# P times V in eight 64x32 tiles over two banks, input sums formed earlier, two gate/up tiles in another phase

## The chip, the cores and the metric

One core of a Trainium2 chip runs the whole program in a single launch. The metric is the device time in microseconds (us), median of three runs. Work is spread over TensorE (matrix products, here PE, with its weight loads as PEld), VectorE (DVE), ScalarE (ACT), GpSimd (POOL) and SyncE (SP), which issues most transfers. Each engine works through its own instruction list in order.

## The reference, cut to what matters

One parallel block over S = 2048 tokens of width D = 640:

```
xn  = layernorm(x)                                   # no scale, no shift
q, k, v = split(xn @ wqkv)                           # 32 heads of 20
p   = softmax(where(0 <= i - j < 256, q k^T / sqrt(20), -1e9))
a   = (p @ v) @ wo                                   # sliding window of 256 tokens
h   = gelu_tanh(xn @ w_gate) * (xn @ w_up)           # 1728 wide
out = x + a + h @ w_down
```

All tensors are float32. The kernel forms the large products from a high and a low part of each operand (fp32r, "h" and "l"), in three products: high by high, low by high, high by low.

## The kernel before, in words

The work is staged as follows.

1. **LayerNorm stage.** Four chunks of 512 tokens are normalised and transposed into `xh` and `xl` (high and low part, five tiles of 128 rows), and V and the first query/key tiles are projected behind them. In this stage the order of work on GpSimd and SP is left to a planner that works from its own costs; the later stages have their order written out by hand on every engine that matters.
2. **Attention** (`attention`, L805). There are 32 units u = (group of 4 heads, chunk of 512 queries). A ramp of 12 slots (numbered -13 to -2) goes ahead of them, then each unit has 14 slots. In a slot the code emits, in order: deferred actions that are due (`tick`), row maxima (`max_pair`, two pairs at slots 0, 4 and 8, and two more after P times V at slot 0), exponentials (`exp_piece`, by the table `SCORES`), GpSimd items from a first-in-first-out list (`release`, up to two), and filler matmuls (`pull_fill`, `RATE`/14 of them a slot). An emitted instruction runs as soon as its inputs and its engine are free; a slot is a place in the order and not a time.
   - The filler (`filler`, L692) projects the remaining query/key and V tiles and computes gate/up tiles densely: 2 x 15 matmuls of 512 columns for each chunk of a tile, so 120 for a tile. `NFA` tiles are done here.
   - `max_pair` (L503) uses 64x32 tiles of the array, two rows of four, with two output banks, and VectorE reduces each bank (L527).
   - `exp_piece` (L568) makes a tile of P, keys by queries, for four heads; `clear` (L588) masks the diagonal and the window's tail on GpSimd (L595, L598). Three such tiles X, Z and Y (`pieces`, L549) belong to a unit.
   - `av_unit` (L601) multiplies P by V for unit u-1 at slot 0 of unit u. Four heads stand side by side as 128x32 tiles of the array, one output bank; ScalarE copies the bank out (L613) and SP stores it.
   - Six PSUM banks form a ring, taken in turn by maxima, exponentials and P times V (`bank`, L498).
   - `x_sums` (L729) forms sums of the normalised input that the next phase needs, for two chunk pairs p. A group of ten GpSimd subtractions and additions of 128x256 (L740) gives four tiles; eight groups are spread, one operation every two slots, over most of the units from slot 24 on. They work in two buffers (tag `tx`), each freed only when its store has landed.
3. **Seven-product phase** (`gate_up_pair`, L935). The remaining gate/up tiles use a Strassen-like scheme: for a pair of chunks 54 matmuls of 512 columns in place of 60.
4. **Down projection and output projection** (L1426 on), which uses a similar scheme.

## Time and profile before

| what | value |
|---|---|
| median of three runs (range) | 1046.38 us (1045.62 to 1047.34) |
| profiled execution, its own time | 1046.71 us |
| its span (first to last instruction) | 1045.0 us |
| granted TensorE clock | 0.999 |
| PE busy / DVE / ACT / POOL | 99% / 69% / 49% / 32% |

Attention takes from about 62 to 570 us of the span, the seven-product phase with its last tile from 570 to about 804 us, and the down projection the rest. Busy shares are averages over these stages. Durations of matmuls in the trace reach from start to a modelled end and overlap; the pitch from one to the next is read from the chain of waits.

### The profile page before, as it was taken

Reading aid. Unit: us, or ns where it says so; the run is one execution under the profiler, and the core shown is the slowest. Engines: PE = TensorE matmul, PEld = TensorE weight load, DVE = VectorE, ACT = ScalarE, POOL = GpSimd, SP = SyncE. Lnnn points to the kernel's source line nnn. Section 1 sums busy time; section 2 is a strip of 40 time slices with the busy share of each in tenths; the row PEclk is TensorE's granted clock in tenths of the full one; section 3 lists DMA queues with packets and bytes.
Section 4 is the critical chain, followed back from the end, with each engine's and each line's share of the span. In section 5 each row is a group of like instructions: output and inputs, shape, how many; then the busy total and the mean of one; then the engine's idle time right before and its main releaser. Section 6 shows DMA issues by size and latency. Waiting matters only on the chain.

```text
span 1045.0 us, 25814 instructions
## 1 busy us (share of the span) xinstructions
PE 1034.0 (99%) x9533; PEld 826.2 (79%) x9533; DVE 717.1 (69%) x2007; ACT 513.6 (49%) x1088; POOL 335.9 (32%) x511
## 2 busy tenths in 40 slices
PE   8999999999999999999999999999999999999998
PEld 8987666666677766666667888888888999999998
DVE  8745656666655556666663678877656888888887
ACT  4444666765665666555656522223324553333332
POOL 5222767766464458464634111110110000000000
PEclk9999999999999999999999999999999999999999
DMA  5552465545332355444322556677217864443342
GB/s 200 189 150 61 136 185 157 174 152 183 98 117 74 106 148 153 129 131 140 103 80 82 191 193 235 220 254 246 100 61 255 272 232 137 136 128 114 124 136 92
DMA packets 105192, 158.76 MB, mean 152 GB/s; under 512 B 15421, under 2 KB 60093, under 8 KB 105065
## 3 DMA queue, kind: packets, MB, share of 16 engines
q1 hardware_dynamic: 102680, 150.95, 45.1%
q10 hardware_dynamic: 2384, 6.16, 1.8%
q8 instruction: 75, 1.23, 0.5%
q14 instruction: 53, 0.43, 0.1%
HBM read 101.78 MB, written 54.92 MB: 150 GB/s over the span
## 4 chain that ended last, share of the span: by engine, by line
PE 89%; DVE 3%; DMA 3%; POOL 2%; SPq 1%; ACT 1%; issue 1%; DVEq 0%; POOLq 0%
PE ps_g L953 21%; PE ps L1220 21%; PE ps_d L110 19%; PE ps_e L582 7%; PE ps_v L110 7%; PE ps_o L609 7%; PE ps_m L523 4%; PE ps_g L110 1%; DMA qs<-qd 1%; SPq L494 1%; PE ps_t L181 1%; DMA qd<-pt 1%; POOL pt L259 1%; PE ps_d L356 1%; POOL wql L643 0%
## 5 line engine op out<-in xcount | busy, mean ns | idle before, releaser
L527 DVE CUSTOM_DVE_ANT_0 junk<-ps_m,mask 128x288 bf16<-128x288 f32 (+2 forms) x512 | 227.9, 445 | 155.0 <-PE ps_m L523 97.2
L584 ACT ACTIVATE P<-ps_e 128x512 f32<-128x512 f32 (+2 forms) x384 | 195.6, 578 | 59.8 <-PE ps_e L582 56.1
L1220 PE MATMUL ps<-wb,at 128*128 128x320 f32 x999 | 155.9, 309 | 0.0
L1220 PEld LDWEIGHTS ps<-wb,at 128*128 128x128 f32 x999 | 148.9, 188 | 0.2
L595 POOL TENSOR_SCALAR_AFFINE_SELECT P<-P 128x512 f32<-128x512 f32 x128 | 84.6, 663 | 139.1 <-ACT P L584 138.1
L582 PE MATMUL ps_e<-qs,ks 124*128 124x128 bf16 (+2 forms) x704 | 107.4, 277 | 0.6 <-DVE mx L527 0.5
L110 PE MATMUL ps_d<-xh,wqh 128*128 128x512 f32 x350 | 104.3, 410 | 0.0
L110 PE MATMUL ps_d<-xl,wqh 128*128 128x512 f32 x350 | 104.3, 409 | 0.0
L110 PE MATMUL ps_d<-xh,wql 128*128 128x512 f32 x350 | 103.9, 409 | 0.0
L1220 PE MATMUL ps<-wt,at 128*128 128x320 f32 x552 | 89.3, 309 | 0.4 <-DVE u L1058 0.4
L582 PEld LDWEIGHTS <-ks 124*128 124x128 bf16 x704 | 50.9, 98 | 46.5 <-issue 29.0
L609 PE MATMUL ps_o<-P,v 128*32 128x384 f32 (+2 forms) x1408 | 84.9, 386 | 0.7 <-POOL P L598 0.7
L1220 PEld LDWEIGHTS ps<-wt,at 128*128 128x128 f32 x552 | 82.9, 188 | 0.9 <-DVE u L1058 0.9
L598 POOL TENSOR_SCALAR_AFFINE_SELECT P<-P 128x512 f32<-128x512 f32 x112 | 70.3, 638 | 33.6 <-ACT P L584 33.6
L1174 ACT ACTIVATE at<-ss 128x512 fp32r<-128x512 f32 x59 | 37.3, 632 | 87.6 <-DVE ss L1058 87.5
L103 POOL TENSOR_TENSOR wql<-wr,wqh 128x640 fp32r<-128x640 f32 x11 | 17.6, 1607 | 174.8 <-PE ps_g L953 149.5
L609 PEld LDWEIGHTS ps_o<-P,v 128*32 128x32 f32 x1408 | 41.0, 109 | 40.5 <-issue 20.4
L110 PEld LDWEIGHTS ps_d<-xh,wql 128*128 128x128 f32 x350 | 63.9, 189 | 11.1 <-issue 0.4
L110 PEld LDWEIGHTS ps_d<-xl,wqh 128*128 128x128 f32 x350 | 63.8, 189 | 10.4 <-issue 0.2
L110 PEld LDWEIGHTS ps_d<-xh,wqh 128*128 128x128 f32 x350 | 63.5, 189 | 10.7 <-issue 0.2
L259 POOL TENSOR_TENSOR pt<-r,pt 128x512 bf16<-128x512 f32 x40 | 46.8, 1169 | 63.2 <-ACT pt L258 63.0
L613 ACT ACTIVATE ob<-ps_o 128x512 f32<-128x512 f32 x32 | 19.1, 598 | 86.3 <-PE ps_o L609 76.1
(194 smaller groups left out, 1846.8 us busy)
## 6 DMA issues: line engine op xcount, KB each, us to landing
hr<-hd SPq DMA_DIRECT2D x104, 128.0 KB
hd<-he SPq DMA_DIRECT2D x50, 256.0 KB
wr<-wgu SPq DMA_DIRECT2D x27, 320.0 KB
qs<-qd SPq DMA_DIRECT2D x64, 120.0 KB
ks<-kd SPq DMA_DIRECT2D x64, 120.0 KB
xi<-x SPq DMA_DIRECT2D x16, 320.0 KB
qs<-qd SPq DMA_DIRECT2D x64, 80.0 KB
ks<-kd SPq DMA_DIRECT2D x64, 80.0 KB
```

Of the source, the lines that this page charges most:

```text
L110: nc.tensor.matmul(ps, a(k), b(k), start=n == 0, stop=n == 3 * nk - 1)
L259: nc.gpsimd.tensor_tensor(out=pt[:, l, :], in0=r, in1=pt[:, 1, :], op=OP.subtract)
L523: nc.tensor.matmul(ps[32 * h:32 * h + 32, lo:hi], q[rows, j, q0:q0 + 32], keys, start=True, stop=True, tile_position=(64 * r, 32 * h))
L527: nc.vector.tensor_tensor_reduce(out=junk[:, 0:n], in0=ps[:, 0:n], in1=mask[:, 288 - n:288], scale=1.0, scalar=NEG, op0=OP.add, op1=OP.max ...
L582: nc.tensor.matmul(ps[:, col:col + n], k[0:QROWS, j, kc:kc + 128], q[0:QROWS, j, q0:q0 + n], start=True, stop=True)
L584: nc.scalar.activation(pt[:, j, lo:hi], ps[:, lo:hi], AF.Exp, scale=SCALE)
L595: nc.gpsimd.affine_select(out=a, in_=a, pattern=[[0, 4], [1, 128]], compare_op=OP.is_ge, fill=0.0, base=0, channel_multiplier=-1)
L598: nc.gpsimd.affine_select(out=a, in_=a, pattern=[[0, 4], [-1, 128]], compare_op=OP.is_ge, fill=0.0, base=-1, channel_multiplier=1)
L609: nc.tensor.matmul(o[32 * j:32 * j + 32, q0:q0 + n], v[:, w0_:w0_ + 32], pt[:, j, col:col + n], start=i == 0, stop=i == len(todo) - 1, ski ...
L953: nc.tensor.matmul(ps, i, j, start=first and n == 0, stop=n == len(work) - 1, skip_group_check=True)
L1174: nc.scalar.activation(hi[:, 3:7], s, AF.Copy)
L1220: nc.tensor.matmul(ps[bank][:, 0:HD], *work[bank][j], start=bank not in begun, stop=final[p, bank] == n and j == len(work[bank]) - 1, skip ...
```

## The change

- **P times V.** The 128 keys of a block become two halves of 64 keys on the two row halves of the array, each half of the sum in a bank of its own: 64x32 tiles, eight at a time. Each half takes only the 320 queries that its 64 keys can see, in place of 384 for 128 keys. The function `windows` pairs a window of the one half with one of the other. ScalarE copies both banks out, the second one into the unit's own P tile, which is no longer needed then; GpSimd adds the two one slot later, and the stores go one slot later too.
- **Sums of the input.** `x_sums` moves up in the file. For the first chunk pair it is called inside the LayerNorm stage (chunks 2 and 3), with two buffers of the tag `he`. For the second pair its 40 operations stand from slot -10 to slot 12, two to a slot; the ramp now releases two items a slot. Stores are deferred by one slot, not four.
- **Gate/up.** `NFA` goes from 4 to 2: two tiles leave the filler and are done in the seven-product phase.
- **Retiming.** `RATE` 34.05 to 26.6 filler matmuls a unit; the second half of V is projected after query/key tile 3; exponentials move from slot 0 to slots 2, 4, 6, 8 and 10.

```diff
-SCORES = {0: range(0, 1), 2: range(1, 5), 4: range(5, 7), 8: range(7, 9), 10: range(9, 12)}
-RATE = 34.05
-V1_AT = "gu", 0, 3
+SCORES = {2: range(0, 3), 4: range(3, 5), 6: range(5, 7), 8: range(7, 9), 10: range(9, 12)}
+RATE = 26.6
+V1_AT = "qk", 3, 3
...
-NFA = 4
+NFA = 2
...
-XS0, XSN = 24, 50
+XS0, XSN = -10, 6
...
+    def x_sums(p, k, half):
...
+            live[i] = (ap.tile([128, w], F32, name="tx", tag="tx") if p else
+                       hp.tile([128, C], F32, name="he", tag="he", bufs=2)[:, 0:w])
...
+            defer(1, lambda: nc.sync.dma_start(td[p][i][:, k, half * w:half * w + w], t))
...
+            if c > 1:
+                for half in range(2):
+                    for fn in x_sums(0, c - 2, half):
+                        fn()
...
+    def windows(c):
+        r = {}
+        for bi, ps in enumerate(pieces(c)):
+            for kb, col, q0, n in ps:
+                for h in range(2):
+                    first = 128 * (kb - 4 * c) + 64 * h
+                    lo = max(0, first) if kb else 0
+                    hi = min(C, first + 320)
+                    r[h, kb - 4 * c] = bi, kb, col + lo - q0, lo, hi - lo
+        pairs = [(0, 0), (-2, -2), (2, -1), (-1, 2), (1, 1), (3, 3)] if c else [(d, d) for d in range(4)]
+        return [[(h, *r[h, d]) for h, d in enumerate(p)] for p in pairs]
+
     def av_unit(u):
         g, c = divmod(u, NC)
-        o, v = bank("ps_o"), vtiles[g]
-        todo = [(pts[u, bi], *p) for bi, ps in enumerate(pieces(c)) for p in ps]
-        for i, (pt, kb, col, q0, n) in enumerate(todo):
-            assert (id(v), kb) in done, (u, kb)
+        halves, v = [bank("ps_o") for _ in range(2)], vtiles[g]
+        todo = windows(c)
+        for i, pair in enumerate(todo):
             for j in range(4):
-                w0_ = kb * 84 + 21 * j
-                nc.tensor.matmul(o[32 * j:32 * j + 32, q0:q0 + n], v[:, w0_:w0_ + 32], pt[:, j, col:col + n],
-                                 start=i == 0, stop=i == len(todo) - 1, skip_group_check=True,
-                                 tile_position=(0, 32 * j))
-        ob = ap.tile([128, C], F32, name="ob", tag="ob", bufs=1)
-        nc.scalar.activation(ob, o, AF.Copy)
+                for h, bi, kb, col, q0, n in pair:
+                    assert (id(v), kb) in done, (u, kb)
+                    rows, w0_ = slice(64 * h, 64 * h + 64), kb * 84 + 21 * j
+                    nc.tensor.matmul(halves[h][32 * j:32 * j + 32, q0:q0 + n], v[rows, w0_:w0_ + 32],
+                                     pts[u, bi][rows, j, col:col + n], start=i == 0, stop=i == len(todo) - 1,
+                                     skip_group_check=True, tile_position=(64 * h, 32 * j))
+        ob, other = ap.tile([128, C], F32, name="ob", tag="ob", bufs=1), pts[u, 2][:, 0, :]
+        nc.scalar.activation(ob, halves[0], AF.Copy)
+        nc.scalar.activation(other, halves[1], AF.Copy)
+        defer(1, lambda: nc.gpsimd.tensor_tensor(out=ob, in0=ob, in1=other, op=OP.add))
...
-        defer(3, store)
+        defer(4, store)
...
-    sets = [("qk", 1), ("qk", 2), ("qk", 3), ("gu", 0), ("qk", 4)]
-    sets += [("gu", f) for f in range(1, NFA)] + [("gu", NF - 1)]
+    sets = [("qk", i) for i in range(1, 5)] + [("gu", f) for f in range(NFA)] + [("gu", NF - 1)]
...
-        for i, (p, k, half) in enumerate((p, k, half) for p in range(NC // 2) for k in range(2) for half in range(2)):
-            for j, fn in enumerate(x_sums(p, k, half)):
-                at(XS0 + XSN * i + 2 * j, when_free, fn)
+        for i, (k, half) in enumerate((k, half) for k in range(2) for half in range(2)):
+            for j, fn in enumerate(x_sums(1, k, half)):
+                at(XS0 + XSN * i + j // 2, when_free, fn)
...
                 pull_max(2, now[0])
             flush()
+            release(2)
             pull_fill(2 * RAMP)
```

More of the change, by code (lines that the diff above doesn't have):

```diff
@@ L421, in first_chunk, with tile_of, pool, store @@
         return w0, w5, mv
+    def x_sums(p, k, half):
+        w = C // 2
+        a, b = (slice((2 * p + i) * C + half * w, (2 * p + i) * C + half * w + w) for i in (0, 1))
+        eh, el = xh.bitcast(F32), xl.bitcast(F32)
+        live = {}
+        def tile_of(i):
+            live[i] = (ap.tile([128, w], F32, name="tx", tag="tx") if p else
+                       hp.tile([128, C], F32, name="he", tag="he", bufs=2)[:, 0:w])
+            return live[i]
+        def pool(o, i, j, op):
+            nc.gpsimd.tensor_tensor(out=o, in0=i, in1=j, op=op)
+        def store(i):
+            t = live[i]
+            defer(1, lambda: nc.sync.dma_start(td[p][i][:, k, half * w:half * w + w], t))
+        def s1():
+            pool(tile_of(1), eh[:, k, b], eh[:, k, a], OP.subtract)
+        def s2():
+            pool(live[1], live[1], el[:, k, b], OP.add)
+        def s3():
+            pool(live[1], live[1], el[:, k, a], OP.subtract)
+            store(1)
+        def s4():
+            pool(tile_of(2), eh[:, k + 2, b], live[1], OP.subtract)
+        def s5():
+            pool(live[2], live[2], el[:, k + 2, b], OP.add)
+            store(2)
+        def s6():
+            pool(tile_of(4), eh[:, k + 2, a], live[2], OP.subtract)
+        def s7():
+            pool(live[4], live[4], el[:, k + 2, a], OP.add)
+            store(4)
+        def s8():
+            pool(tile_of(3), eh[:, k + 2, b], eh[:, k, b], OP.subtract)
+        def s9():
+            pool(live[3], live[3], el[:, k + 2, b], OP.add)
+        def s10():
+            pool(live[3], live[3], el[:, k, b], OP.subtract)
+            store(3)
+        return s1, s2, s3, s4, s5, s6, s7, s8, s9, s10
     v0 = []
```

38 lines of the change are left out of this document (removed).

## The prediction, made before the changed kernel was timed

> **What bounds the kernel now.** I read the page's busy shares first, then the stages in windows, then the chain of waits.
>
> ```profile
> PE 1034.0 (99%) x9533; PEld 826.2 (79%) x9533; DVE 717.1 (69%) x2007; ACT 513.6 (49%) x1088; POOL 335.9 (32%) x511
> ...
> PE 89%; DVE 3%; DMA 3%; POOL 2%; SPq 1%; ACT 1%; issue 1%; DVEq 0%; POOLq 0%
> ```
>
> ```profile
> 62.00:570.00 508.00, 504.23 (x6479) 341.20 (x6478) 299.20 (x1169) 308.27 (x681) 286.53 (x445) 1.00 0.43 129
> 570.00:804.00 234.00, 234.00 (x1035) 193.76 (x1034) 165.61 (x275) 77.17 (x143) 24.90 (x17) 1.00 0.55 189
> ```
>
> The columns of the windows are span, then busy time of PE, PEld, DVE, ACT and POOL. TensorE is busy in attention and in the seven-product phase alike, at the full clock, so a product that is saved is worth its own time, as long as nothing else comes late. The second view of the same fact is the chain in order of time, here a stretch of attention and the seven-product phase (start, length, what):
>
> ```profile
> 101.64 0.63 ACT pt L258
> 102.27 1.47 ACT P L584 x3
> ...
> 103.80 0.64 POOL P L595
> 104.44 0.60 POOL P L598
> ...
> 105.08 1.07 PE ps_o L609 x16
> ...
> 115.96 2.28 PE ps_d L110 x10
> 118.24 0.36 PE ps_m L523 x20
> 118.61 2.75 PE ps_o L609 x48
> 121.35 0.37 PE ps_m L523 x16
> ...
> 583.30 220.37 PE ps_g L953 x972
> ```
>
> Matmul follows matmul, with one exception to keep in mind: at 102 to 105 us, the end of unit 0, P times V waits for exponentials (ACT) and then for GpSimd's masks. Whatever makes GpSimd late at that place is paid in full.
>
> **The change, part by part.**
>
> *A. Two gate/up tiles move.* The filler loses 2 x 120 matmuls at 2.28/10 = 0.228 us: 54.7 us. The seven-product phase gains 2 x 2 x 54 = 216 at 220.37/972 = 0.2267 us: 49.0 us. Gain 5.7 us. Their weight loads, vector work and stores move with them into a stage where DVE is busy 166 of 234 us, so I cost these at nothing; if that cover failed, a tile's matmuls would still be 24.5 us each.
>
> *B. P times V.* A unit with c > 0 streams 12 passes (a float32 product takes two) over 1536 x 2 = 3072 columns in 2.75 us: 0.895 ns a column. The new pairs stream the longer of two windows: 320+128+256+192+320+128 = 1344, twice 2688 columns, 2.41 us; if the two halves can run apart, each has 1280, that is 2.29 us. For c = 0 it is 1152 before and 1088 (or about 1024) after. Saved: 24 x 0.34 + 8 x 0.11 = 9.1 us at the least, 24 x 0.46 + 8 x 0.23 = 12.9 us at the most; I take 11. This supposes that eight 64x32 tiles run side by side. The row maxima already work so:
>
> ```profile
> 512.17 0.32 PE L523 MATMUL ps_m<-ks,qs 60*32 60x288 bf16 x8
> ...
> 512.17 0.44 PE L523 MATMUL ps_m<-ks,qs 60*32 60x288 bf16 x16
> ...
> 509.06 0.45 PE L523 MATMUL ps_m<-ks,qs 60*32 60x32 bf16 x32
> ...
> 512.17 0.14 PEld L523 LDWEIGHTS <-qs 60*32 60x32 bf16 x16 [0.20 <-issue]
> ```
>
> The first eight end 0.12 us before the second eight (0.44 - 0.32): 288 columns in 0.12 us is the time of one stream, so eight did run at once, over two row halves and two banks. Matmul count itself is cheap: 32 took 0.45 us where 16 with the same columns in all took 0.44. The Trainium skill speaks against the change here: "TensorEngine Tiling (Array Packing)", section Instruction Overhead, gives some 60 cycles for every matmul and says that a dimension which is already small should give no tiling factor. By 60 cycles at 2.4 GHz, 25 ns, the 32 matmuls above would take 0.8 us; the trace has 0.45, so I don't follow it in the sum, and keep it as a rival.
>
> *C. Fewer changes of tile shape.* P times V is emitted between two bursts of maxima. Before, the shapes are 64x32, 128x32, 64x32; after, all three are 64x32. The last row above shows what a change costs: the weight loader sat idle 0.20 us, with nothing to wait for, before the maxima that follow P times V; some 0.1 us of it is the last pass still streaming (128 columns at 0.895 ns). Two such borders a unit at 0 to 0.1 us: 0 to 6.4 us over 32 units; I take 0.15 us a unit, 4.8 us. (The skill's same page, Key Properties, says that a change of tiling mode drains the engine; the idle 0.20 us agrees.)
>
> *D. The sums, ahead of the units.* Rows for GpSimd, from lists of single lines and from the timeline:
>
> ```profile
> L740 POOL TENSOR_TENSOR tx<-tx,xl x48: 723/733/1109, 121.0 to 513.9; 128x256 f32<-128x256 f32 x48
> ...
> 27.94 3.03 DVE L190 TENSOR_TENSOR xl<-ps_t,xh 128x512 fp32r<-128x512 f32 x5
> ...
> 40.02 0.61 POOL L467 MEMSET xi<- 128x288 f32 x2 [1.24 <-PE ps_t L181]
> ...
> 45.72 0.44 POOL L473 COPY mask<-xi 32x288 f32<-32x288 f32 x1
> ...
> 68.65 1.17 POOL L259 TENSOR_TENSOR pt<-r,pt 128x512 bf16<-128x512 f32 x1 [9.32 <-ACT pt L258]
> 69.77 3.09 POOL L103 TENSOR_TENSOR wql<-wr,wqh 128x640 fp32r<-128x640 f32 x2
> ...
> 103.62 1.28 PE L609 MATMUL ps_o<-P,v 128*32 128x384 f32 x16
> ```
>
> Follow GpSimd's list from slot -10 to the masks of tile Y of unit 0, which stand at slot 11. It holds 4 low parts of projections (1.17 us), the two low weights (3.09), 36 of the second pair's 40 operations (0.74 each, 26.6) and the 6 masks of unit 0 (0.6 apart, 3.6): 38 us. It cannot start before 68.65, when the first of them has its input; so it ends at 106.7 without a single wait. TensorE wants the masks earlier than that: P times V stood at 103.62, unit 0 loses 7.45 filler matmuls (1.7 us), and the first pair of windows (384 columns, two passes) takes 0.7: 102.6. GpSimd is 4 us late, and TensorE, which works in order, stands. To this come the waits for buffers: each group of ten reuses its two buffers four times, and the store must have landed:
>
> ```profile
> POOL tx L740 <- DMA td<-tx: 4.8, 3, 4.3
> ...
> PEld ps_o L609 <- POOL P L598: 3.8, 13, 1.0
> ...
> PEld ps_o L609 <- POOL P L595: 1.9, 4, 0.7
> ...
> PEld ps_o L609 <- POOL tx L740: 1.2, 6, 0.2
> ```
>
> (waiter, releaser: total us, times, longest). 1.6 us a wait at a looser spacing; with one a group not hidden, 4 x 1.3 = 5 us. I take 9 us. Ends: GpSimd's whole work from 28.5 us, when the first pair's inputs exist, is masks 5, eight low parts 9.4, weights 3.1, 76 operations 56, masks of unit 0 3.6: 77 us, done at 105.6 if it never pauses, so 3 us is the least. The most: of the 40 us between 28.5 and 68.65 some 30 are free, and the first pair needs 29.6 plus 4 waits of 1.6; 6 us spill over, 16 in all. Queued behind the late masks are the last four sums, their stores, and behind these on SP the loads of unit 3's queries; they come due at slot 4 of unit 1 and are inside the upper end. What moves out of the units frees GpSimd of 80 x 0.74 / 32 = 1.9 us a unit and takes away the six waits of the last row: gain 1 us.
>
> *E. The tail of P times V and the ring.* New on GpSimd is the addition, 128x512, between 1.17 us (the subtraction above) and two 128x256 (1.48 us), less than the 1.9 freed, and one more ScalarE copy:
>
> ```profile
> L613 ACT ACTIVATE ob<-ps_o 128x512 f32<-128x512 f32 x32 | 19.1, 598 | 86.3 <-PE ps_o L609 76.1
> ...
> 512.55 0.46 DVE L527 CUSTOM_DVE_ANT_0 junk<-ps_m,mask 128x288 bf16<-128x288 f32 x1 [0.80 <-PE ps_m L523]
> ...
> 513.16 0.46 DVE L527 CUSTOM_DVE_ANT_0 junk<-ps_m,mask 128x288 bf16<-128x288 f32 x1
> ```
>
> 0.6 us on an engine that is busy 308 of 508 us; ScalarE and GpSimd hide both. What they do not hide is that a unit gets shorter, about 15.8 to 13.7 us, while VectorE's sixteen maxima at a pitch of 0.61 us stay (9.8 us, with the rest some 11.5). Exponentials at slot 6 now take the banks of maxima from slot 4. TensorE gets there after 0.37 (maxima) + 0.35 (two exponentials) + 0.87 (two slots of 1.9 fillers) + 0.1 = 1.7 us, and the third maximum is reduced after 1.83: a wait of 0.1 us when VectorE is free, 0.8 when one operation of 0.7 us stands before it. Also the time between the last exponentials and Y's masks shrinks by 4 x 0.12 us of filler and 0.23 of earlier windows, where 5.7 us of waits are seen now (17 times). Between 0 and 0.5 us a unit, 0 to 16 us; I take 5, near the seen waits.
>
> *Sum.* -5.7 - 11 - 4.8 + 9 - 1 + 5 = -8.5 on a span of 1045.0: 1036.5. The profiled execution took 1046.71, 1.7 more than its span, and lies 0.3 above the median: about 1038.
>
> **The rivals.**
>
> *R1, slower: VectorE and the ring bind.* Place: slots 6 and 8 of every unit. It decides from (22.5 - 9)/32 = 0.42 us a unit. With 0.8 us, one other vector operation before the maxima each time, it is 26 us: 1059. For it: some 11.5 of 13.7 us of VectorE in a unit, and only six banks. Against: VectorE still waited for maxima (0.80 in the row above) and fillers stand between.
>
> *R2: GpSimd is not late, or TensorE regains it, and the ring holds.* D and E at their low ends: 1046.4 - 22.5 + 3 = 1027. Against it: the in-order count above.
>
> *R3: the burst eats the gain.* D at 16, with E at 5: 1045; no change to be told. For it: the chain already runs through GpSimd at 103.80.
>
> *R4: the eight don't run side by side*, because float32 differs from the maxima's bf16: P times V then takes 4.6 us a unit, 57 us lost: above 1100. R5: a floor per matmul, the skill's page above. With 25 ns, a pass of eight takes at least 0.2 us; the passes over 128 and 192 columns (0.115 and 0.172 us) grow, 0.4 us a unit, 10 us in all: 1048.
>
> **How the numbers follow.** Forecast 0.46 (own range 1032 to 1044), R2 0.20 (1023 to 1032), R3 0.14 (1043 to 1050), R1 0.14 (1049 to 1063), R4 0.03, R5 0.03. All terms at their low ends give 1024, at their high ends 1063. With 1026 to 1053 some 0.16 is left out. A measurement of this kernel tells 0.2%, 2.1 us, from no change: faster is below 1044.3, forecast, R2 and a little of R3, 0.70; slower above 1048.5, R1 and R4, 0.17; between 0.13.
>
> **What would show it.** A: the seven-product phase holds 1188 matmuls at about 0.227 us. B: P times V of a unit takes 2.3 to 2.4 us on the chain; 2.75 or more refutes B, and two separate groups of four would show R4. C: the idle time of the weight loader beside P times V goes below 0.1 us. D: TensorE waits for a mask (L595 or L598 of before) once, at 102 to 112 us, for 3 to 16 us, with GpSimd busy from 70 us on; no such wait refutes D. E: waits of scores or exponentials on the vector engine's maxima, each under a microsecond, 5 us in all; over 13 us gives R1. The forecast is wrong if neither D nor E is seen, or if attention shrinks by less than 50 us of its 508.

## The result: 1075.4 us, 2.7% slower, and the profile after

The changed kernel takes 1075.41 us (median of four runs, 1074.54 to 1075.85) against 1046.72 for the kernel before, timed beside it: a ratio of 1.0274, 95% interval 1.0256 to 1.0292. The forecast was 1038 us. The profiled execution took 1074.54 us with a span of 1072.8, 27.8 us longer than before.

The page of the changed kernel, busy shares, chain and granted clock:

```profile
PE 1037.1 (97%) x10917; PEld 852.0 (79%) x10917; DVE 731.3 (68%) x2029; ACT 523.1 (49%) x1120; POOL 374.7 (35%) x527
...
PEclk9989999999999999999999999999999999999999
...
PE 82%; DVE 5%; POOL 4%; DMA 4%; ACT 3%; issue 2%; SPq 1%; DVEq 0%; ACTq 0%; POOLq 0%
```

TensorE's share of the chain fell from 89% to 82%, and one of the forty slices, the one in which attention starts, no longer has the full clock. The chain of waits at the end of attention gives the split by stage (start, length, what), here the first piece after attention in the kernel before, and then in the changed one:

```profile
569.65 13.65 PE ps_g L110 x60
```

```profile
548.10 13.92 PE ps_g L110 x60
562.02 269.47 PE ps_g L973 x1188
```

Attention ends at 548.10 where it ended at 569.65: 21.5 us earlier, and the forecast had 57.5. The rest of the kernel is 49.4 us longer, and the forecast had 49.0. So all of the miss lies in attention. The windows of the changed kernel (span, then busy time of PE, PEld, DVE, ACT, POOL, then granted clock) show where TensorE is idle:

```profile
62.00:548.00 486.00, 459.04 (x7653) 327.65 (x7651) 286.16 (x1149) 304.59 (x691) 303.53 (x438) 0.98 0.43 128
...
62.00:82.00 20.00, 12.15 (x88) 9.39 (x87) 6.33 (x21) 4.37 (x14) 16.38 (x23) 0.74 0.39 123
98.00:108.00 10.00, 7.34 (x67) 6.93 (x67) 3.88 (x16) 2.29 (x13) 9.36 (x12) 0.83 0.65 199
122.00:130.00 8.00, 5.97 (x93) 3.80 (x101) 3.91 (x12) 2.66 (x5) 7.46 (x10) 0.79 0.42 120
```

The first of the short windows in the kernel before:

```profile
62.00:82.00 20.00, 20.00 (x210) 15.82 (x209) 10.17 (x45) 6.19 (x19) 5.39 (x4) 1.00 0.52 158
```

TensorE was busy for all of its 20 us, with 210 matmuls at the full clock; now it holds 88. In all three short windows GpSimd (the fifth busy time) works for 82 to 94% of the time. The chain and the lists of single lines say who waits for whom. Chain of the changed kernel:

```profile
67.91 0.73 POOL he L435
69.45 2.23 DMA ks<-kd
71.82 0.51 PE ps_m L581 x15
72.33 6.04 PE ps_d L110 x16
78.74 3.40 PE ps_d L110 x14
...
112.42 0.64 POOL P L653
...
121.76 0.73 POOL tx L435
122.48 0.59 POOL P L653
123.07 0.60 POOL P L656
123.72 1.58 PE ps_o L680 x38
```

SyncE's queue and TensorE in the timeline of the changed kernel; brackets give the idle time before an instruction and what ended it:

```profile
67.05 1.94 SPq L439 DMA_DIRECT2D td<-he  x2
69.05 1.11 SPq L552 DMA_DIRECT2D ks<-kd  x3
71.98 1.84 SPq L439 DMA_DIRECT2D td<-he  x2
73.87 1.10 SPq L552 DMA_DIRECT2D qs<-qd  x3
```

```profile
71.82 0.52 PE L581 MATMUL ps_m<-ks,qs 60*32 60x32 bf16 x27 [7.85 <-DMA ks<-kd]
...
100.66 1.51 PE L110 MATMUL ps_v<-wvh,xh 128*128 128x320 f32 x5 [2.82 <-DVE r L273]
...
123.72 1.59 PE L680 MATMUL ps_o<-P,v 64*32 64x320 f32 x47 [3.03 <-POOL P L656]
```

What SyncE itself waited for from 44 to 84 us (waiter, releaser: us in total, times, longest):

```profile
SPq L439 <- POOL he L435: 19.3, 14, 3.9
```

Read together: the sums of the first chunk pair (tile `he`, L435) run on GpSimd in the LayerNorm stage, from 27.5 to 81.3 us. Each store of a sum (L439) waits on SP's queue for GpSimd. Behind these stores, in the same queue, stand the loads of the first keys and queries (L552). These loads wait for nothing of their own: the last three for the first keys are issued at 69.05 us, as soon as the store ahead of them is out, where the kernel before had issued all six by 49.0. TensorE stands 7.85 us, and its score matmuls go on at 71.8 us; before, the first ones came at 62.4. The 16 filler matmuls after that take 6.04 us, 0.378 us each on average, where 0.228 is normal: the clock records have a granted share of 0.50 from 66.8 to 77.0 us. At 100 us VectorE's `r` (L273) has waited 5.5 us for GpSimd, and TensorE waits for `r`; at 123 us TensorE waits for GpSimd's masks. Each time the clock drops again. The first P times V starts at 119.7 us; before it started at 103.6.

The other thing to see is P times V itself (chain pieces, then the weight loads of the first):

```profile
305.92 3.00 PE ps_o L680 x61
...
332.77 2.21 PE ps_o L680 x60
```

```profile
306.40 1.95 PEld L680 LDWEIGHTS ps_o<-P,v 64*32 64x32 f32 x84 [0.53 <-DVE mx L585]
```

Where nothing is in its way, a unit's P times V takes 2.21 us on the chain, and 2.27 from its first matmul to the next instruction. In 18 of the 32 units P times V or its weight load waits for VectorE to read one of the four maxima that stand just ahead of it in the same slot, 8.2 us in all. So one of its two banks was last used by such a maximum, and P times V takes up to 2.9 us or starts up to 0.65 us behind the last maximum instead of 0.06.

### The profile page after: what moved, and what is told of

Read it like the earlier page. It is cut to its first block, busy times and chain, and to the rows that moved or that the text cites. A ratio compares the mean times of both kernels' runs of the same rounds, so it can differ in the third digit from the quotient of the medians.

```text
span 1072.8 us, 28727 instructions
## 1 busy us (share of the span) xinstructions
PE 1037.1 (97%) x10917; PEld 852.0 (79%) x10917; DVE 731.3 (68%) x2029; ACT 523.1 (49%) x1120; POOL 374.7 (35%) x527
## 4 chain that ended last, share of the span: by engine, by line
PE 82%; DVE 5%; POOL 4%; DMA 4%; ACT 3%; issue 2%; SPq 1%; DVEq 0%; ACTq 0%; POOLq 0%
PE ps_g L973 25%; PE ps L1240 20%; PE ps_d L110 12%; PE ps_e L640 7%; PE ps_o L680 6%; PE ps_v L110 5%; PE ps_m L581 3%; DVE junk L585 2%; DMA qs<-qd 2%; ACT P L642 1%; POOL he L435 1%; PE ps_g L110 1%; POOL tx L435 1%; POOL pt L259 1%; DMA ks<-kd 1%
## 5 line engine op out<-in xcount | busy, mean ns | idle before, releaser
L680 PE MATMUL ps_o<-P,v 64*32 64x320 f32 (+5 forms) x2816 | 85.8, 349 | 5.0 <-POOL P L656 3.6
L110 PE MATMUL ps_d<-xh,wql 128*128 128x512 f32 x270 | 85.9, 424 | 0.0
L110 PE MATMUL ps_d<-xh,wqh 128*128 128x512 f32 x270 | 85.4, 422 | 0.0
L110 PE MATMUL ps_d<-xl,wqh 128*128 128x512 f32 x270 | 83.8, 415 | 0.0
L581 PE MATMUL ps_m<-ks,qs 60*32 60x96 bf16 (+5 forms) x3008 | 68.1, 246 | 16.1 <-DMA ks<-kd 7.8
L680 PEld LDWEIGHTS ps_o<-P,v 64*32 64x32 f32 x2816 | 62.7, 106 | 22.8 <-DVE mx L585 6.8
L581 PEld LDWEIGHTS <-qs 60*32 60x32 bf16 x3008 | 34.3, 90 | 51.2 <-issue 43.9
L1002 ACT ACTIVATE hr<-hr 128x512 f32<-128x512 f32 x22 | 13.9, 632 | 111.4 <-DVE hr L976 111.4
L973 PE MATMUL ps_g<-xl,wqh 128*128 128x512 f32 x198 | 66.3, 389 | 0.0
L973 PE MATMUL ps_g<-xh,wqh 128*128 128x512 f32 x198 | 66.3, 389 | 0.0
## 6 DMA issues: line engine op xcount, KB each, us to landing
hr<-hd SPq DMA_DIRECT2D x104, 128.0 KB
```

Source lines behind the costliest of these rows:

```text
L110: nc.tensor.matmul(ps, a(k), b(k), start=n == 0, stop=n == 3 * nk - 1)
L581: nc.tensor.matmul(ps[32 * h:32 * h + 32, lo:hi], q[rows, j, q0:q0 + 32], keys, start=True, stop=True, tile_position=(64 * r, 32 * h))
L680: nc.tensor.matmul(halves[h][32 * j:32 * j + 32, q0:q0 + n], v[rows, w0_:w0_ + 32], pts[u, bi][rows, j, col:col + n], start=i == 0, stop=i ...
L973: nc.tensor.matmul(ps, i, j, start=first and n == 0, stop=n == len(work) - 1, skip_group_check=True)
```

## The experiments

All runs below the first row were timed in three rounds (w5 in five) beside the kernel before, which had medians of 1046.0 to 1046.3. "End" is the end of attention in the profiled execution. That execution was the longest of its run in e1, e4, e5 and y2, 2.3 to 3.8 us above the median, and in w1 1.5 us below it, so "end" and what is read from these traces are off by about as much.

| run | what it is | us (range) | ratio, 95% interval | end |
|---|---|---|---|---|
| after | the change | 1075.4 (1074.5 to 1075.9) | 1.0274 [1.0256, 1.0292] | 548.1 |
| e2 | before + early sums | 1065.4 (1064.1 to 1069.2) | 1.0186 [1.0158, 1.0214] | 588.4 |
| e8 | before + second pair early | 1052.9 (1052.3 to 1054.2) | 1.0068 [1.0051, 1.0084] | 575.1 |
| e1 | after, sums as before | 1073.6 (1070.0 to 1077.4) | 1.0259 [1.0230, 1.0289] | 549.5 |
| e3 | before + P times V | 1052.6 (1051.0 to 1053.0) | 1.0055 [1.0040, 1.0070] | 574.1 |
| e5 | e3 + new slots of exponentials | 1048.9 (1048.0 to 1052.5) | 1.0035 [1.0020, 1.0049] | 572.7 |
| e10 | after, P times V as before | 1076.3 (1074.4 to 1077.3) | 1.0286 [1.0270, 1.0301] | 550.2 |
| e9 | after, P times V ahead of maxima | 1109.9 (1109.6 to 1112.1) | 1.0613 [1.0597, 1.0629] | 582.9 |
| e4 | before + two tiles moved | 1062.1 (1059.6 to 1064.5) | 1.0149 [1.0126, 1.0171] | 538.3 |
| e7 | e4, sums late | 1051.2 (1050.0 to 1051.7) | 1.0046 [1.0031, 1.0061] | 524.4 |
| y2 | e4, sums spaced | 1051.8 (1050.8 to 1054.0) | 1.0048 [1.0033, 1.0063] | 527.8 |
| x_pvgu_late | after, sums late | 1066.1 (1065.2 to 1066.7) | 1.0190 [1.0175, 1.0205] | 539.5 |
| y1 | after, sums spaced | 1058.3 (1056.1 to 1061.9) | 1.0117 [1.0096, 1.0137] | 532.0 |
| w2 | e5, sums late | 1046.0 (1044.4 to 1049.2) | 0.9999 [0.9988, 1.0011] | 567.6 |
| w1 | e5, sums spaced | 1042.1 (1040.5 to 1045.4) | 0.9965 [0.9955, 0.9975] | 563.3 |
| w5 | before, sums spaced | 1043.8 (1043.2 to 1045.0) | 0.9976 [0.9966, 0.9986] | 566.0 |

### The early sums: e2, e8, e1

**e2_sums_only.** The kernel before with the change's two edits to the sums (the first pair in the LayerNorm stage, the second ahead of the units):

```diff
-XS0, XSN = 24, 50
+XS0, XSN = -10, 6
...
+            if c > 1:
+                for half in range(2):
+                    for fn in x_sums(0, c - 2, half):
+                        fn()
...
-                at(XS0 + XSN * i + 2 * j, when_free, fn)
+                at(XS0 + XSN * i + j // 2, when_free, fn)
...
```

> The kernel before with the early sums alone (P times V, the gate/up split and the exponentials' slots as before). Theory S: 20 us slower than before, 1060 to 1070, and the same waits for key loads and masks in the first 125 us. The prediction's step D alone (only the burst of GpSimd ahead of unit 0's masks, 9 us): 1055.

Measured: 1065.4, 19.4 us over the kernel before, as theory S had it. Waits of TensorE in this run (waiter, releaser: us in total, times, longest):

```profile
PE ps_m L581 <- DMA ks<-kd: 7.8, 1, 7.8
PE ps_o L679 <- POOL P L656: 4.6, 1, 4.6
PE ps_v L110 <- DVE r L273: 3.6, 2, 3.0
```

The first P times V starts at 119.2 us, the next 22.2 us later where 14.9 is normal, and the units after that are as before. The prediction's step D, 3 to 16 us, is only in the second row. The first row, the largest, stands at a place that the prediction had not considered.

**e8_second_pair_early.** The same with only the second pair early; the first pair is spread over the units, nothing is added to the LayerNorm stage. The edit against e2:

```diff
-            if c > 1:
-                for half in range(2):
-                    for fn in x_sums(0, c - 2, half):
-                        fn()
...
+        for i, (k, half) in enumerate((k, half) for k in range(2) for half in range(2)):
+            for j, fn in enumerate(x_sums(0, k, half)):
+                at(24 + 50 * i + 2 * j, when_free, fn)
```

> The kernel before with only the second pair's sums ahead of the units, as the changed kernel has them; the first pair's sums are spread over the units as before, none stand in the layernorm stage. With both early 1065.4 us were measured, 19.4 more than before. Theory L (most of the loss comes from the first pair: its stores stand on SP's queue ahead of the loads of the first keys, TensorE stands 8 us and then has half the clock for 10 us): the first score matmuls come when they came in the kernel before, and what is left is GpSimd's lateness for the masks of unit 0, 3 to 8 us and perhaps one more stretch of half clock: 1050 to 1056 us. Rival D (the burst ahead of unit 0's masks is the loss, as the prediction has it, and larger): 1060 to 1066 us, with the same waits for GpSimd's masks and about 3 units that start late.

Measured: 1052.9, 6.7 us over. Theory L holds. Waits and a window:

```profile
PE ps_o L674 <- POOL P L651: 4.6, 1, 4.6
```

```profile
110.00:114.00 4.00, 2.88 (x35) 1.15 (x36) 0.47 (x2) 0.60 (x1) 3.84 (x7) 0.50 0.60 167
```

One wait for the mask of unit 0, at 106 to 111 us, is step D as predicted. The clock records have 0.50 from 108.2 to 115.0 us, so that the four microseconds behind the wait run at half clock, which costs some 2 us: together with the wait's 4.6 that is the 6.7. The other 12.5 us of the 19.4 come with the first pair in the LayerNorm stage. That they come through SP's queue is read from the queue's own waits above; the queue alone was not changed in any run.

**e1_sums_back.** The changed kernel with the sums spread over the units as before.

```diff
-XS0, XSN = -10, 6
+XS0, XSN = 24, 50
...
-            if c > 1:
-                for half in range(2):
-                    for fn in x_sums(0, c - 2, half):
-                        fn()
...
```

> The changed kernel with the sums of the input placed as before (all eight groups spread over the units). Theory S (the early sums hold up the start: in the trace of the changed kernel the first P times V comes at 119.7 to 123.7 us, 20 us after the 103.6 of before, with a wait of 7.9 us for the first key loads, 3.0 us for masks, 2.8 us behind a vector operation, and half-clock stretches): about 1055 us, 1052 to 1058, with the granted clock back at 1.0 near the start. Rival (the start is lost for another reason, or is made up later): 1070 or more.

Measured: 1073.6, the rival's 1070 or more. The theory that the place of the sums explains the miss falls here as far as it was a sum of parts: the start is right again, but stretches of half clock appear at 168, 199 and 404 us instead, and TensorE's waits for the queries' loads rise from 4.8 to 10.2 us. With the sums in the units something else is as dear. The next runs look for it.

### P times V: e3, e5, e10, e9

**e3_pv_only.** The kernel before with the new `windows` and `av_unit`, nothing else.

```diff
-        o, v = bank("ps_o"), vtiles[g]
+        halves, v = [bank("ps_o") for _ in range(2)], vtiles[g]
...
-                                 tile_position=(0, 32 * j))
+                                     skip_group_check=True, tile_position=(64 * h, 32 * j))
```

> The kernel before with P times V in eight 64x32 tiles alone. The prediction's steps B, C and E: 11 us faster, 1035. Theory R (the second bank of P times V is taken from maxima of the same slot, which VectorE has not reduced, and the ring runs short elsewhere): the saving is eaten and more; from the stretch 124 to 548 us of the changed kernel, which is 42 us shorter than its counterpart where the moved filler alone is 53 us, it would be 11 us slower, 1052 to 1060.

Measured: 1052.6, 6.5 us over, the lower end of theory R. P times V does get shorter, 83.4 to 72.1 us over all units (summing, over the trace, the time from each of its matmuls to the next matmul), the 11 us of step B. It comes back as a new wait:

```profile
PE ps_e L582 <- ACT ob L626: 9.2, 21, 0.5
```

The first exponential stood at slot 0, right behind P times V, and now takes a bank that ScalarE is still copying out: two copies instead of one. By the same sums the time at the maxima, in which these waits lie, grows by 13.9 us; what the rest of it waits for was not taken apart.

**e5_pv_slots.** That plus the change's slots, where exponentials begin at slot 2.

```diff
-SCORES = {0: range(0, 1), 2: range(1, 5), 4: range(5, 7), 8: range(7, 9), 10: range(9, 12)}
+SCORES = {2: range(0, 3), 4: range(3, 5), 6: range(5, 7), 8: range(7, 9), 10: range(9, 12)}
```

> The kernel before with P times V in eight tiles and with the slots of the maxima as the changed kernel has them (first maxima at slot 2, exponentials taken from there), nothing else changed. In P times V alone 1052.5 us were measured against 1046.0, and the trace showed 9.2 us of waits of the first exponential for the bank that ScalarE copies out, and the maxima's share grown by 14 us. Theory Q (the place of the copies decides): with the slots moved the 9 us go, and the 11 us by which P times V itself got shorter show: 1040 to 1044 us. Rival R (a bank taken from maxima of the same slot decides, wherever the maxima stand): P times V or the maxima still wait about 0.5 us a unit, 16 us in all: 1048 to 1054 us. The wait of the first exponential for ScalarE's copy falls below 1 us in both.

Measured: 1048.9. The 9.2 us are gone, as both theories had it, and the time is rival R's. In the profiled execution, which took 1052.5, most units are shorter, 14.6 us for 15.0, but one takes 20.6. Timeline of this run, GpSimd, then VectorE, then TensorE:

```profile
398.95 0.74 POOL L755 TENSOR_TENSOR tx<-xh,tx 128x256 f32<-128x256 f32 x1 [2.28 <-DMA td<-tx]
...
402.71 0.69 DVE L273 TENSOR_TENSOR r<-ps_d,pt 128x512 f32<-128x512 f32 x1 [3.64 <-POOL pt L259]
...
403.82 2.08 PE L622 MATMUL ps_o<-P,v 64*32 64x384 f32 x62 [1.53 <-DVE mx L527]
...
411.05 0.17 PE L523 MATMUL ps_m<-ks,qs 60*32 60x32 bf16 x1 [1.71 <-DVE r L273]
```

A sum on GpSimd waits for the store that frees its buffer; the low part `pt` queued behind it is late; VectorE stands 3.64 us for it with the maxima queued behind; and TensorE stands for VectorE, 1.53 us at P times V and, with VectorE still behind, another 1.71 us at 411. Then follow 3.4 us at half clock. P times V's extra addition had made GpSimd's list longer; that this is why the chain forms is argued and not shown. Two of the six executions, 1048.0 and 1048.3, had a mean granted clock of 1.000, so this half clock does not come in every execution. The next test of the chain is w1.

**e10_no_pv.** The changed kernel with the old P times V.

```diff
-        halves, v = [bank("ps_o") for _ in range(2)], vtiles[g]
+        o, v = bank("ps_o"), vtiles[g]
```

> The changed kernel with P times V in four tiles over one bank as before; the early sums, the two moved tiles and the slots of the maxima stay. Theory S (in units this short P times V's shorter streams are lost to waits for banks): 1073 to 1079 us, that is at most 4 us more than the 1075.4 of the changed kernel. Rival A (P times V is worth its 9 to 12 us plus the shape changes): 1085 to 1091 us.

Measured: 1076.3, 0.9 us more than the changed kernel, intervals overlapping. Theory S holds: in the changed kernel the eight tiles are worth about nothing. From the fourth unit on, P times V takes 5.7 us less in the changed kernel than here (by the same sums over the trace), and the maxima 4.4 us more.

**e9_after_av_first.** The changed kernel, P times V emitted ahead of the maxima of slot 0, so that none of its banks belongs to a maximum of that slot.

```diff
-                if i in BURSTS:
-                    pull_max(2, T)
                 if i == 0 and u:
                     av_unit(u - 1)
                     flush()
                     pull_max(2, T)
+                if i in BURSTS:
+                    pull_max(2, T)
```

> The changed kernel with one difference: at slot 0, 4 and 8 the matmuls of P times V are emitted ahead of that slot's maxima instead of behind them, so that no bank of P times V was last used by a maximum of the same slot. In the changed kernel 19 of 32 units have such a bank, and their P times V takes 2.9 us or starts late, about 0.64 us a unit. Theory B (the bank decides): these waits go and P times V takes 2.3 us in every unit, 19 x 0.64 = 12 us: 1061 to 1066 us. Rival O (VectorE is the limit, and the wait only shows at P times V): the same time waits elsewhere, at the exponentials or the next maxima, 1072 to 1077 us. A third way: the changes of slot order leave the maxima later by P times V's 2.3 us and it is slower, over 1080 us.

Measured: 1109.9. P times V takes 2.27 us in most units, as it should without the banks' wait, and a typical unit is 14.5 us instead of 13.4. Waits of the changed kernel and of this one:

```profile
DVE junk L585 <- PE ps_m L581: 90.8, 89, 7.8
```

```profile
DVE junk L585 <- PE ps_m L581: 123.4, 54, 9.4
...
PE ps_m L581 <- ACT ob L684: 10.2, 30, 0.4
...
PE ps_e L640 <- DVE mx L585: 7.0, 26, 0.5
```

This is the third way of the expectation. Theory B had the bank's wait right and its price wrong: with P times V first, the maxima wait for ScalarE's copy once a unit (30 times), VectorE gets them later by P times V, and the exponentials wait for VectorE. The wait at P times V was only where the six banks ran out first.

### The two tiles: e4, e7, y2

**e4_gu_only.** The kernel before with the two tiles moved.

```diff
-RATE = 34.05
-V1_AT = "gu", 0, 3
+RATE = 26.6
+V1_AT = "qk", 3, 3
-NFA = 4
+NFA = 2
-    sets = [("qk", 1), ("qk", 2), ("qk", 3), ("gu", 0), ("qk", 4)]
-    sets += [("gu", f) for f in range(1, NFA)] + [("gu", NF - 1)]
+    sets = [("qk", i) for i in range(1, 5)] + [("gu", f) for f in range(NFA)] + [("gu", NF - 1)]
```

> The kernel before with the two gate/up tiles moved alone (filler rate and the place of V's second half go with it). The prediction's step A: 5.7 us faster, 1040.7 (1039 to 1042). Rival (units with less filler run into VectorE): no gain or slower, 1046 or more.

Measured: 1062.1, 16 us over: the rival, 1046 or more. The seven-product phase is longer by what step A said, 49.2 us; attention is shorter by 31.4 us, not 54.7. Most units take 13.5 us for 15.0, close to the 1.7 us that 7.5 matmuls less should give, but four take 17.9, 15.8, 20.0 and 16.6. The timeline of this run in the first of them, VectorE and then GpSimd, and the list of all the instructions of that VectorE line (shortest/median/longest, ns):

```profile
135.34 4.11 DVE L536 TENSOR_SCALAR nm<-mx 128x16 bf16<-128x16 f32 x1
```

```profile
131.66 1.17 POOL L259 TENSOR_TENSOR pt<-r,pt 128x512 bf16<-128x512 f32 x1
132.78 0.74 POOL L739 TENSOR_TENSOR tx<-tx,xl 128x256 f32<-128x256 f32 x1
...
138.70 0.73 POOL L739 TENSOR_TENSOR tx<-tx,xl 128x256 f32<-128x256 f32 x1
141.01 1.16 POOL L259 TENSOR_TENSOR pt<-r,pt 128x512 bf16<-128x512 f32 x1 [1.58 <-ACT pt L258]
```

```profile
L536 DVE TENSOR_SCALAR nm<-mx x32: 174/175/4114, 77.6 to 516.4; 128x16 bf16<-128x16 f32 x32
```

GpSimd runs from 128.0 to 139.4 without a gap: masks, low parts, sums, and the low parts of weights, which the shorter units now bring closer together. A VectorE operation of 0.175 us takes 4.11 in that time and ends when GpSimd does; TensorE waits 2.68 us behind it and then has half the clock.

**e7_gu_late_sums.** The same, sums from slot 168 on.

```diff
-XS0, XSN = 24, 50
+XS0, XSN = 168, 30
```

> The two gate/up tiles moved (with the places of the weights of V that belong to it), as in the run that did only this, but the sums of the input start at slot 168 and come 30 slots apart, instead of at 24 and 50 apart. Theory C (GpSimd is crowded in units 2 to 7, where weights, masks and sums meet, and TensorE then stands and is granted half the clock): the four units of 16 to 20 us become units of 13.5 to 15; of the 21 us between 1062 and the forecast 1040.7 at least 12 come back: 1041 to 1050 us, with no stretch at half clock before 200 us. Rival V (VectorE and the ring cannot go at 13.5 us a unit, whatever GpSimd does): 1058 to 1064 us, the long units somewhere else.

Measured: 1051.2, just over theory C's 1050; 10.9 us come back where it had at least 12, and no unit is longer than 15.2 us. Chain of this run:

```profile
524.38 13.66 PE ps_g L110 x60
```

Attention is 45.3 us shorter here, the nearest that any run comes to the 54.7 of step A. The 9.4 us that are missing are spread thin: by the sums over the trace the exponentials take 4.9 us more than before and the maxima 4.9 more.

**y2_gu_spread.** e4 with the ten steps of a group of sums 4 slots apart instead of 2.

```diff
-                at(XS0 + XSN * i + 2 * j, when_free, fn)
+                at(XS0 + XSN * i + 4 * j, when_free, fn)
```

> The two gate/up tiles moved and nothing else but the steps of the sums 4 slots apart: against the 1062.1 us with steps 2 apart and the 1051.2 with groups late. Theory C (close steps make the crowds): 1044 to 1052 us, the units of 17.9, 15.8, 20.0 and 16.6 us fall to 15 and less. Rival W (the weights of V and of the projections, not the sums' spacing, make the crowd in units 2 to 7): 1056 to 1063 us.

Measured: 1051.8, in theory C's range, and the long units are 15.9 us at most. Late groups (e7) and steps further apart bring back about the same, 10.9 and 10.3 us: it is enough that the sums do not meet the weights and masks of units 2 to 7 in one crowd.

### All parts, and a kernel faster than both: x_pvgu_late, y1, w2, w1, w5

**x_pvgu_late** and **y1_all_spread**: the change with the sums back in the units (as in e1), placed as in e7 and spaced as in y2:

```diff
-XS0, XSN = 24, 50
+XS0, XSN = 168, 30
...
-                at(XS0 + XSN * i + 2 * j, when_free, fn)
+                at(XS0 + XSN * i + 4 * j, when_free, fn)
```

The first two lines are x_pvgu_late's against e1, the last two y1's.

> The changed kernel in everything but the sums: they are spread over the units again, from slot 168 on and 30 slots apart (before: 24 and 50), so that they neither stand ahead of the first units nor fall on units 2 to 8, where two sets of weights are split. Theory S (the place of the sums is worth some 25 us of the changed kernel: 16 at its first P times V, 5.5 in its unit 0 to 1, 4 in its unit 4 to 5; and with units of 13.4 us P times V's gain is lost to other waits): 1048 to 1053 us, no better than the two gate/up tiles with late sums alone (1051.2). Rival A (the gains add up: 1051.2 less 9 to 12 for P times V): 1039 to 1043 us. Third: sums and the extra addition crowd GpSimd again and units of 17 us and more appear: over 1060 us.

> The changed kernel in P times V, slots and the two moved tiles, with the sums in the units from slot 24 on, 50 apart, and their steps 4 slots apart. With groups from slot 168, 30 apart and steps 2 apart 1066.1 us were measured, with units of 17.8 and 17.3 us and 8 us of waits for queries. Theory C (crowds on GpSimd, made by steps close together, are the cost): the long units go, units of 13.3 to 13.6 us all along: 1046 to 1053 us. Rival U (a unit of 13.4 us has no room for 80 sums, 32 additions and the weights, however they are spaced): 1058 to 1068 us. No better than 1042 in either, since seven-product matmuls cost 49 of the 54.7 us that the filler loses.

Measured: 1066.1 and 1058.3. The first is the third case, long units again (17.8 and 17.3 us) with 7.9 us of waits for queries. The second lies at the lower end of rival U: one unit of 17.7 us is left, most others take 13 to 14.5, and it is 6.5 us slower than y2, which has the old P times V and slots. With units this short, the eight tiles and their slots cost time. Against the changed kernel the two placements are worth 9 and 17 us, and no placement tried makes all its parts pay.

**w2_pv_late and w1_pv_spread**: e5 with the late sums and with the spaced sums (edits as in e7 and y2).

> The same as the run before in this list but for the sums: two slots apart again, the groups from slot 168 on and 30 apart. In the kernel with the two moved tiles this took 11 us off. Theory Q: the crowds move to other units; if none of the new places is worse, 1040 to 1045 us. Rival R: 1046 to 1050 us. If the sums' groups now meet the last units' weights, a long unit shows between units 12 and 28 and it is over 1050 us.

> P times V in eight tiles with the changed kernel's slots for the maxima, on the kernel before, as in the run that measured 1048.9 us; the only difference to that run: the ten steps of a group of sums come 4 slots apart instead of 2, so that a step does not wait on GpSimd for the store that frees its buffer. That run lost 6 us in unit 20 to 21, where GpSimd stood 2.3 us for such a store, VectorE 3.6 us for GpSimd and TensorE 4 us for VectorE and late queries, and then ran 3.4 us at half clock. Theory Q (that one crowd is the difference to the forecast): it goes, 1040 to 1044 us, faster than the kernel before. Rival R (waits for banks spread over all units eat it): 1046 to 1050 us.

Measured: 1046.0 and 1042.1. w2 is at the lower end of rival R. w1 is theory Q: the long unit is gone (14.8 us), and the kernel is faster than before, by 0.35%. Waits of w1:

```profile
PEld ps_o L622 <- DVE mx L527: 4.5, 9, 0.5
...
PEld L544 <- DVE mx L527: 3.8, 14, 0.3
```

**w5_before_spread**: the kernel before with the spaced sums alone.

> The kernel before, its ten steps of a group of sums 4 slots apart instead of 2, nothing else: how much of the 1042.1 us measured with P times V and this spacing belongs to the spacing. Theory P (P times V makes the gain, the spacing only removes the crowd that P times V's extra addition brought): 1044.5 to 1047 us, as before. Rival X (the spacing itself makes the gain, and P times V is worth nothing): 1040 to 1043 us.

Measured: 1043.8, faster than before by itself and so between the two expectations. Of w1's 4 us the spacing has 2.4. For P times V with its slots 1.2 us (by the ratios) to 1.7 us (by the medians) remain, with intervals that overlap (0.9955 to 0.9975 and 0.9966 to 0.9986), so that this last gain is likely and not shown. In the traces w1's P times V takes 8.6 us less than w5's from the fourth unit on, and the maxima take 4.6 us more: even here half of it is handed on.

## Why the prediction was wrong, by its steps

By the profiles, the span came out 36.3 us above the forecast of 1036.5. Attention can be cut at the fourth P times V (149.4 us before, 166.1 after). Up to there the forecast had +9 from D and three units shorter by 2.1, +2.8 in all; the trace has +16.7: a miss of 13.9. From there to the end of attention 29 units were to save 60.3 us and saved 38.3: a miss of 22.0. Behind attention the miss is 0.4.

Two steps failed. The sum took the TensorE time saved in A, B and C as time saved in the unit, with the other engines at nothing in A and at 5 us in E. And D put the first pair's stores on SP's queue at nothing. The second failure is the miss at the start. For the first an estimate from the runs: of B's and C's 15.8 us e10 found 0.9 in the changed kernel, some 15 us short, and of A's 54.7 us attention lacked 9.4 even with the sums out of the way (e7). That makes 24 us, about the 22.

- **A, seven-product term (+49.0): right.** 1188 matmuls in 269.47 us, 0.2268 each, 49.1 us more.
- **A, filler term (−54.7): wrong**, and with it the sentence that the tiles' surroundings cost nothing. Only TensorE's time was moved in that sum. It asked for cover in the phase that the tiles go to, and not in the units that they leave. In the run with only this edit and the old spacing attention shrank by 31.4 us, with the sums late by 45.3. GpSimd's and VectorE's work per unit stays while the unit gets shorter, and where weights, masks and sums meet the cover fails.
- **B (−11): the size was right, what followed from it was not.** 2.27 us a unit against a forecast of 2.29 to 2.41, and 11 us less in all in e3. So rival R4 is out. R5 is out by the narrow passes: in the changed kernel's trace the last eight matmuls of a unit's P times V, over 64 and 128 columns, start within 0.11 us, 14 ns each. The Trainium skill's "TensorEngine Tiling (Array Packing)", Instruction Overhead, the rule of some 60 cycles for a matmul behind R5, is not what this trace shows. The mean over a unit, 96 matmuls in 2.27 us or 23.6 ns each, lies too near to R5's 25 ns to decide it. But 11 us less of P times V was worth 0.9 us, within the noise, in the changed kernel (e10), a loss beside y2, and perhaps 1.2 to 1.7 us where units have room (w1 against w5).
- **C (−4.8): the front border is right, the row behind it was read too simply.** Where nothing else waits, the first matmul of P times V comes 62 ns behind the last maximum instead of 178: 0.116 us in each of 30 units, 3.5 us. At the border behind P times V the weight loader's idle 0.20 us is gone too; its loads now run into one another (weight loader of the changed kernel):

```profile
332.54 2.23 PEld L680 LDWEIGHTS ps_o<-P,v 64*32 64x32 f32 x90
334.66 0.09 PEld L581 LDWEIGHTS <-qs 60*32 60x32 bf16 x1
```

  But the step took that idle time for the price of a change of shape, and the old P times V has the same 0.19 us of it up to four times inside a unit, where no shape changes. These are its waits before and after:

```profile
PEld ps_o L609 <- issue: 20.4, 104, 0.4
```

```profile
PEld ps_o L680 <- issue: 3.5, 7, 0.7
```

  So how much of it belongs to the shape stays open. It is no gain on top of B either: the 2.75 and 2.27 us of a unit reach to the next instruction and hold this border already, some 0.19 us x 30 = 5.7 of B's 11 us.
- **D (+9, 3 to 16): the mechanism was right and inside its range, a larger one beside it was missed.** Alone it costs 6.7 us (e8), of which the wait is 4.6. The step counted the first pair's 40 operations on GpSimd as time that fits into a gap but for 6 us at the most, and their 16 stores on SP as nothing; it had SP's queue in mind for the second pair alone. The first pair's sums last to 81.3 us, 12.6 behind the 68.65 at which the step lets the second pair's list begin. Their stores wait on SP for GpSimd, and SP holds the first keys behind them: 12.5 us more (e2 less e8). The step also left out the clock. In the changed kernel the clock records show 20.5 us at half. TensorE worked in 15.4 of them, so that some 7.7 us were lost, an estimate.
- **E (+5, 0 to 16): inside its range, wrong in the place.** The waits that it named are as forecast: TensorE waits for maxima 2.6 us at the maxima and 2.1 at the exponentials. Not counted were those of P times V and its weight load, 8.2 us. The step had the exponentials of slots 6 and 8 in mind. P times V with its two banks out of six meets the maxima of its own slot first. The step's unit of 15.8 us was the whole of attention over 32; from one P times V to the next it was 15.0 before and is 13.4 now, a little shorter than the 13.7 that the step reckoned with. Rival R1, in which the ring binds, described the loss of B better than the forecast did, with the wrong slots and too small a chance.
- **−1 for the sums that leave the units:** in short units their place is worth far more than that (e4 against e7 and y2: 10 to 11 us), and this is the likely reason why the parts do not add. Measured alone, sums +19.4, tiles +16.0 and P times V with its slots +2.6 make 38.0; together they cost 28.7. The early sums take their crowd out of units 2 to 7 and pay for it at the start: the fifth to the seventh unit take 18.8, 17.1 and 18.8 us in e1 and 17.2, 13.0 and 13.6 in the changed kernel, and yet the two kernels differ by only 1.8 us.

The prediction named what would refute it: attention shrinking by less than 50 us. It shrank by 21.5.

What stays open: how w1's remaining wait at the banks would go with a different order of maxima (e9 tried one and was worse), and whether SP's queue alone, with the first pair's sums left where the change puts them, is all of the 12.5 us. Open too is how much of C belongs to the change of shape.

## What to carry to other kernels

Moving matmuls off TensorE shortens the unit for every engine: count what each of them still does per unit, and look for the places where their bursts meet, before taking the matmuls' time as the gain. A store that waits for a slow engine, put into an in-order queue ahead of a load, delays the load by the engine's backlog, here by some 20 us. And where buffers or banks are few, a shorter user of them hands its time to the next one unless there are banks to spare; spacing out the small work (4 slots for 2) was worth 2.4 us by itself, and the new product perhaps 1.2 to 1.7 on top.

## What the runs showed of the hardware

- **A short stall costs more than itself.** In the changed kernel the clock records have a granted share of 0.50 from 66.77, 100.90, 124.80 and 189.65 us on, for 3.41 us each, the first for 10.24; the ten filler matmuls from 72.3 to 76.7 us took 0.44 us each instead of 0.228. These starts lie whole multiples of 3.41 us apart. In the 3.41 us ahead of each start TensorE has no matmul in the records for 2.80, 2.82, 2.33 and 1.69 us; of the other such pieces at full clock, from 5 to 1070 us, none has more than 1.21. So half of a piece is enough: the last start follows waits of only 1.54 and 0.71 us for queries. The Trainium skill's "TensorE: Matmul & The Clock Gate", Part 1, has the clock halved after an idle window of about 3.4 us. The length agrees with this trace; that the window has to be idle throughout does not.
- **GpSimd can hold up VectorE without a semaphore.** An operation on 16 columns, 0.175 us in the median, took 4.11 us in a stretch in which GpSimd ran without a gap, and the maxima ahead of it, which read PSUM, kept their pace. The Trainium skill's "GPSIMD Engine Reference", Specifications, says that the two share their SBUF interfaces, and that VectorE instructions in a two-port mode or with two SBUF inputs contend. The trace agrees with that; no run here shows which mode it was.
- **Eight 64x32 float32 tiles run side by side**, over two row halves and two banks: 1280 columns of each half, two passes, in 2.27 us, the 0.9 ns a column of the four tiles before.
